# Loading K of the second attention unit in two halves, in a sliding-window attention kernel on one core

## The chip, the cores and the metric

The kernel runs on one core of one Trainium2 chip. The metric is the device time of one execution in microseconds; lower is better. Four runs of the kernel before gave 184.63, 184.4, 185.11 and 186.37 us, median 184.87 us.

## The reference, cut to what matters

```python
B, Sq, D = 8, 32, 1024
Hq, Hkv, Sk, Dh = 32, 4, 8192, 128
W = min(4096, max(256, Sk // 4))            # 2048: only the last W keys are used
rep = Hq // Hkv                             # 8 query heads share one K/V head
q = (x @ wq).reshape(B, Sq, Hq, Dh).transpose(0, 2, 1, 3)
k = repeat(k_cache[:, :, Sk - W:, :], rep, axis=1)
v = repeat(v_cache[:, :, Sk - W:, :], rep, axis=1)
scores = einsum("bhqd,bhkd->bhqk", q, k) * Dh ** -0.5
p = softmax(scores, axis=-1)
o = einsum("bhqk,bhkd->bhqd", p, v)
return o.transpose(0, 2, 1, 3).reshape(B, Sq, Hq * Dh) @ wo
```

All inputs are bfloat16. The K and V that are used come to 32 pairs of 2048 x 128, 512 KB each.

## The kernel before, in words

**Units.** One unit is one batch row b and one K/V head g; there are 32, head by head, so units 0 to 7 are the eight batch rows of head 0. A unit has 256 query rows (8 heads times 32) and 2048 keys, cut into 16 tiles of 128 keys. It is worked in four chunks of four key tiles. A chunk is four matmuls for scores (`s_ps`, L504), one exponential on ScalarE (`pT`, L506), and eight matmuls of the probabilities with V (`o_ps`, L515). The V tile `va` carries a column of ones, so that the sum of the softmax comes out of the same matmuls. The V matmuls of a chunk are issued two chunks after its scores. Four chunks of 32 units give 128 slots; other work is dealt out to slots: the query projection of later heads (`q_ps`, L285, and `ql_ps`, L301), the output projection (`op_ps`, L322) and the turning of some K.

**K must be turned.** The scores need K with Dh on the partitions (`kT`). There are three ways. Units 0, 1 and 2 (`PE_T`) load K as it lies into `k_raw` and turn it on TensorE (L397 for unit 0, `tp` at L244 for units 1 and 2); VectorE copies each half of eight tiles out of PSUM (L401, L246). Units in `V_T` (4, 7, 9, 12 and so on) load K as it lies and turn it with VectorE block transposes (`kb`, L259) and block moves on VectorE and GpSimd (`kTv`, L268 and L270). All others use a transposing DMA, in two halves (L200). In this text K1 is K of unit 1, V1 is V of unit 1, and so on; wq is the query weight.

**Where K1 is turned.** The pieces for K1 are placed among the chunks of unit 0: the first half (tiles 0 to 7) after the scores of chunk 2, the second half after those of chunk 3. K2's pieces lie in unit 1, after chunk 1, 2 and 3.

**Loads.** All loads but one half of x are issued by SyncE's queue, in the order of the program. `start` writes the first of them out by hand: x, six pieces of wq with the two halves of K0 among and behind them, V0, K1, V1, K2, K4, V2, and then unit 3: first half of K3, V3, second half of K3. From then on `load_unit` is called at a slot for each unit.

**Completion semaphores.** In the program as it is built, DMAs take eight completion semaphores in turn, and a DMA that reuses one waits on the issuing queue until the transfer that had it before has landed. So every DMA waits for the transfer eight issues before it, and everything behind it in SyncE's queue waits too. In the kernel before, V1 waits for the fourth piece of wq, K2 for the fifth, K4 for the first half of K0, V2 for the sixth piece of wq, the first half of K3 for the seventh, V3 for the second half of K0, and the second half of K3 for V0.

**Copies of V.** V lands in `v_sb` and is copied into one of three `va` buffers: for units 1 and 2 by GpSimd (L437), for all others by VectorE (L439).

**VectorE's order.** VectorE works in the order of the program. Around unit 1 it is: the two copies of K1 (L246), the first block transpose of K4 (L259), the closing of unit 0 (L445, L449, L451), the copy of K2's first half (L246), two more block transposes of K4, the copy of K2's second half, and so on.

Of the kernel before, what the change touches and what calls it, by code (L numbers as in the profile page):

```python
# [108 lines left out]
class Fast:  # L109
# [229 lines left out]
    def start(self):  # L339
# [14 lines left out]
        wq0[6]()  # L354
        self.load_k(0, 1)
        self.load_v(0, nc.sync)
        self.load_k(1)
        self.weights = []
        for g in range(self.Hkv):
            if g + 1 < self.Hkv:  # L360
# [333 lines left out]
```

## Time and profile before

| what | value |
|---|---|
| median of four runs | 184.87 us |
| the profiled execution, its own time | 184.98 us |
| its span in the profile | 183.2 us |
| PE busy | 178.0 us, 97% of the span |
| PEld busy | 152.8 us, 83% |
| ACT, DVE, POOL busy | 136.1, 125.5, 89.2 us |
| granted TensorE clock | 1.0 |
| data moved by DMA | 51.72 MB, mean 282 GB/s |
| the chain that ended last | PE 93%, DMA 4% |

The span is the time from the first to the last recorded instruction. The profiled execution took 1.78 us more than its span, and 0.11 us more than the median. PE is TensorE's matmuls, PEld its weight loads, DVE VectorE, ACT ScalarE, POOL GpSimd, SPq the queue of SyncE that issues DMAs. A DMA's row in the timeline is the time that its issuing takes; when the data has landed is told apart from it, as a time from issue to landing.

### The profile page before, as it was taken

Reading aid. Unit: us, or ns where it says so; the run is one execution under the profiler, and the core shown is the slowest. Engines: PE = TensorE matmul, PEld = TensorE weight load, DVE = VectorE, ACT = ScalarE, POOL = GpSimd, SP = SyncE. Lnnn points to the kernel's source line nnn. Section 1 sums busy time; section 2 is a strip of 40 time slices with the busy share of each in tenths; the row PEclk is TensorE's granted clock in tenths of the full one; section 3 lists DMA queues with packets and bytes.
Section 4 is the critical chain, followed back from the end, with each engine's and each line's share of the span. In section 5 each row is a group of like instructions: output and inputs, shape, how many; then the busy total and the mean of one; then the engine's idle time right before and its main releaser. Section 6 shows DMA issues by size and latency. Waiting matters only on the chain.

```text
span 183.2 us, 5015 instructions
## 1 busy us (share of the span) xinstructions
PE 178.0 (97%) x2026; PEld 152.8 (83%) x2041; DVE 125.5 (69%) x257; ACT 136.1 (74%) x146; POOL 89.2 (49%) x138
## 2 busy tenths in 40 slices
PE   8989999999999999999999999999999999999994
PEld 2879999999999999997878899988777788888843
DVE  0228799689887698477898656867587987554253
ACT  2218889888797888998787787788777788888800
POOL 2001665069880695945949706929705949600000
PEclk9999999999999999999999999999999999999999
DMA  5999999989999999999999997999999999970013
GB/s 187 320 407 406 231 378 381 245 261 261 363 393 253 358 262 342 381 281 324 292 381 246 415 359 257 383 243 354 277 302 275 339 292 338 209 176 0 0 32 89
DMA packets 52953, 51.72 MB, mean 282 GB/s; under 512 B 39744, under 2 KB 40256, under 8 KB 52928
## 3 DMA queue, kind: packets, MB, share of 16 engines
q1 hardware_dynamic: 52352, 50.90, 97.8%
q10 hardware_dynamic: 576, 0.49, 0.9%
q8 instruction: 15, 0.25, 0.5%
q14 instruction: 10, 0.08, 0.1%
HBM read 41.42 MB, written 0.52 MB: 229 GB/s over the span
## 4 chain that ended last, share of the span: by engine, by line
PE 93%; DMA 4%; SPq 1%; issue 1%; DVE 0%
PE o_ps L515 32%; PE s_ps L504 31%; PE op_ps L322 14%; PE q_ps L285 11%; DMA wq_sb<-in_wq_dram 4%; PE q_ps L405 2%; PE ql_ps L301 1%; PE tp L244 1%; SPq L168 1%; PE kf_ps L397 0%; SPq L347 0%; DVE o_t L332 0%; PE cnt_ps L570 0%
## 5 line engine op out<-in xcount | busy, mean ns | idle before, releaser
L506 ACT ACTIVATE pT<-s_ps 128x1024 bf16<-128x1024 f32 x128 | 128.4, 1027 | 26.8 <-PE s_ps L504 26.6
L270 POOL TENSOR_SCALAR kTv<-kb 32x512 bf16<-32x512 bf16 x126 | 84.5, 670 | 51.3 <-DVE kb L259 33.1
L515 PE MATMUL o_ps<-va,pT 128*128 128x129 bf16 x1024 | 78.8, 220 | 0.1
L515 PEld LDWEIGHTS <-pT 128*128 128x128 bf16 x1024 | 68.5, 98 | 3.1
L504 PE MATMUL s_ps<-QT,kT 128*128 128x256 bf16 x336 | 50.4, 272 | 0.1
L504 PEld LDWEIGHTS <-kT 128*128 128x128 bf16 x336 | 31.9, 98 | 9.4
L322 PE MATMUL op_ps<-wo_sb,OT 128*128 128x512 bf16 (+2 forms) x129 | 32.9, 353 | 0.6
L259 DVE STREAM_TRANSPOSE kb<-k_raw 128x512 bf16<-128x512 bf16 x44 | 29.7, 691 | 1.2 <-DMA k_raw<-in_k_cache_dram 0.9
L285 PE MATMUL q_ps<-xT,wq_sb 128*128 128x256 bf16 x192 | 28.3, 273 | 0.0
L504 PE MATMUL s_ps<-QT,kTv 128*128 128x256 bf16 x176 | 26.4, 273 | 0.1
L439 DVE COPY va<-v_sb 128x2048 bf16<-128x2048 bf16 x30 | 25.1, 835 | 1.1 <-DMA v_sb<-in_v_cache_dram 0.6
L445 DVE RECIPROCAL RL_all<-o_ps 128x2 f32<-128x2 f32 x32 | 5.3, 166 | 27.7 <-PE o_ps L515 27.3
L268 DVE COPY kTv<-kb 32x512 bf16<-32x512 bf16 x50 | 22.6, 452 | 1.2
L504 PEld LDWEIGHTS <-kTv 128*128 128x128 bf16 x176 | 17.0, 98 | 6.1
L285 PEld LDWEIGHTS <-wq_sb 128*128 128x128 bf16 x192 | 16.9, 98 | 1.2
L451 DVE STREAM_TRANSPOSE OT<-o_sb 128x256 bf16<-128x256 bf16 x32 | 14.3, 446 | 1.1
L449 DVE TENSOR_TENSOR o_sb<-o_ps,RL_all 128x256 bf16<-128x256 f32 x32 | 13.6, 424 | 1.1
L322 PEld LDWEIGHTS <-OT 128*128 128x128 bf16 x144 | 11.3, 98 | 2.3
L437 POOL TENSOR_SCALAR va<-v_sb 128x2048 bf16<-128x2048 bf16 x2 | 3.8, 1897 | 17.8 <-DMA v_sb<-in_v_cache_dram 17.8
L288 ACT CAST QT<-q_ps 128x512 bf16<-128x512 f32 x12 | 7.0, 582 | 0.2 <-PE q_ps L285 0.2
L405 PE MATMUL q_ps<-xT,wq_sb 128*128 128x256 bf16 (+1 forms) x64 | 6.0, 247 | 0.8 <-DMA wq_sb<-in_wq_dram 0.8
L329 DVE TENSOR_TENSOR oacc<-op_ps,oacc 128x512 f32<-128x512 f32 x8 | 5.3, 662 | 2.0 <-PE op_ps L322 2.0
(35 smaller groups left out, 43.6 us busy)
## 6 DMA issues: line engine op xcount, KB each, us to landing
v_sb<-in_v_cache_dram SPq DMA_DIRECT2D x30, 512.0 KB, 6.7
wo_sb<-in_wo_dram SPq DMA_DIRECT2D x16, 512.0 KB, 6.5
wq_sb<-in_wq_dram SPq DMA_DIRECT2D x13, 512.0 KB, 6.9
k_raw<-in_k_cache_dram SPq DMA_DIRECT2D x13, 512.0 KB, 6.0
wq_sb<-in_wq_dram SPq DMA_DIRECT2D x6, 256.0 KB, 5.4
v_sb<-in_v_cache_dram SPq DMA_DIRECT2D x4, 256.0 KB, 4.6
kT<-in_k_cache_dram SPq DMA_TRANSPOSE x36, 7.1
k_raw<-in_k_cache_dram SPq DMA_DIRECT2D x2, 256.0 KB, 6.9
```

The source lines that it names most:

```text
L259: nc.vector.transpose(out=st["kb"][:, sl, :], in_=self.k_raw[ui][:, sl, :])
L268: nc.vector.tensor_copy(out=out, in_=in_)
L270: nc.gpsimd.tensor_scalar(out=out, in0=in_, scalar1=1.0, scalar2=1.0, op0=ALU.mult, op1=ALU.mult)
L285: nc.tensor.matmul(st[k][:, hl % 2, :], lhsT=self.wq_t[g, i][:, c % (DC // 2), hl * P:(hl + 1) * P], rhs=self.xT[:, c, :], start=(c == 0 a ...
L322: nc.tensor.matmul(ps[:, 0:w], lhsT=self.OT[:, gq, c, t * P:(t + 1) * P], rhs=self.wo_t[gq][:, c, n0:n0 + w], start=(k == 0), stop=(k == 7))
L405: nc.tensor.matmul(ps, lhsT=self.wq_t[0, c // H][:, c % H, h * P:(h + 1) * P], rhs=self.xT[:, c, 0:n], start=(c == 0 and h in (0, 2, 4)), ...
L439: self.nc.vector.tensor_copy(out=out, in_=in_)
L449: nc.vector.tensor_tensor(out=o_sb[:, :, :, :], in0=o_ps[:, :, 0:Dh].rearrange("p q (i c) -> p q c i", c=4), in1=rl[:, ui * QT_N:(ui + 1) ...
L451: nc.vector.transpose(out=self.OT[:, g * QT_N:(g + 1) * QT_N, :, b * self.Sq:(b + 1) * self.Sq], in_=o_sb[:, :, :, :])
L504: nc.tensor.matmul(s_ps[:, jj, :], lhsT=self.kT[ui][:, c * CJ + jj, :], rhs=q_u, start=True, stop=True)
L506: nc.scalar.activation(out=pT[:, :, :], in_=s_ps[:, :, :], func=ACT.Exp, bias=0.0, scale=self.scale)
L515: nc.tensor.matmul(o_ps[:, qt, 0:self.VW], lhsT=pT[:, jj, qt * P:(qt + 1) * P], rhs=va[:, j, 0:self.VW], start=(j == 0 and qt == 0), stop= ...
```

## The change

K1 is issued as two loads of 256 KB, tiles 0 to 7 and tiles 8 to 15, into the two halves of the same `k_raw` buffer. `load_k` already has the form with a part: K0 uses it.

```diff
@@ -354,7 +354,8 @@
         wq0[6]()
         self.load_k(0, 1)
         self.load_v(0, nc.sync)
-        self.load_k(1)
+        self.load_k(1, 0)
+        self.load_k(1, 1)
         self.weights = []
```

The code that turns K1 is not touched. In the built program the eight matmuls that turn the first half of K1 now wait for the first of the two loads alone, and those for the second half have a wait of their own for the second. SyncE's queue has one DMA more, so every DMA behind K1 takes the next semaphore in the turn: V1 now waits for what K2 waited for, K2 for what K4 waited for, and so on. The order of the instructions on all engines is otherwise the same.

## The prediction

> **What bounds the kernel now.** I read the table of busy time first, then the table of waits for PE and PEld, then the stretches of 1 us at the start, then SyncE's own timeline with the landing time of each load, and last VectorE's timeline around unit 1.
>
> ```profile
> PE 178.0 (97%) x2026; PEld 152.8 (83%) x2041; DVE 125.5 (69%) x257; ACT 136.1 (74%) x146; POOL 89.2 (49%) x138
> ...
> PE 93%; DMA 4%; SPq 1%; issue 1%; DVE 0%
> ```
>
> ```profile
> PE q_ps L405 <- DMA wq_sb<-in_wq_dram: 0.8, 1, 0.8
> PE warm_ps L375 <- PEq L678: 0.8, 1, 0.8
> ```
>
> PE is busy nearly all the time, and its list of waits has two lines: 0.8 us before the first instruction, and 0.8 us for a piece of wq. Nothing in it names k_raw, so PE never waited for K1. The stretches (window, clock, busy time of PE, PEld, DVE, ACT, POOL, clock, DMA share, GB/s) show where the second wait lies, and that DMA runs at its full rate while K1 is on its way:
>
> ```profile
> 9.00:10.00 1.00, 0.27 (x5) 0.10 (x2) 0.00 (x0) 0.00 (x0) 0.00 (x0) 1.00 1.05 401
> ...
> 16.00:17.00 1.00, 1.00 (x19) 0.99 (x18) 1.00 (x3) 1.00 (x2) 0.00 (x0) 1.00 1.00 389
> 17.00:18.00 1.00, 1.00 (x18) 0.97 (x16) 0.70 (x2) 0.75 (x2) 0.42 (x1) 1.00 1.00 401
> ```
>
> From 10.1 us on PE is full in every stretch that I read (to 45 us). So a microsecond of PE stall is a microsecond of time, and little can be won: at most the 0.8 us at 9 to 10 us, which waits for a piece of wq issued 4.3 us ahead of K1.
>
> Now the loads. SyncE's timeline (start, duration of issue, line):
>
> ```profile
> 7.40 0.55 SPq L197 DMA_DIRECT2D k_raw<-in_k_cache_dram  x1
> 8.41 0.33 SPq L208 DMA_DIRECT2D v_sb<-in_v_cache_dram  x1
> 10.09 1.01 SPq L197 DMA_DIRECT2D k_raw<-in_k_cache_dram  x2
> 11.43 0.33 SPq L208 DMA_DIRECT2D v_sb<-in_v_cache_dram  x1
> 12.12 1.35 SPq L200 DMA_TRANSPOSE kT<-in_k_cache_dram  x1
> 13.52 4.47 SPq L208 DMA_DIRECT2D v_sb<-in_v_cache_dram  x1
> 18.04 3.13 SPq L200 DMA_TRANSPOSE kT<-in_k_cache_dram  x1
> ```
>
> These are K1, V1, K2 with K4, V2, the first half of K3, V3, the second half of K3. The answer by tile, cut to the window of one issue, gives the time to landing of each; issue plus that is: V0 6.80 + 7.3 = 14.1; K1 7.40 + 7.9 = 15.3; V1 8.41 + 9.1 = 17.5; K2 10.09 + 8.6 = 18.7; K4 about 10.8 + 9.1 = 19.9; V2 11.43 + 9.8 = 21.2; half of K3 12.12 + 10.0 = 22.1. Of the 7.9 us of K1, only some 1.3 us is its own data (512 KB at 400 GB/s). The rest is queueing behind what was issued before.
>
> Last, who takes the data. In the timeline of all engines:
>
> ```profile
> 16.33 0.49 PEld L244 LDWEIGHTS <-k_raw 128*128 128x128 bf16 x8
> ...
> 17.58 1.90 POOL L437 TENSOR_SCALAR va<-v_sb 128x2048 bf16<-128x2048 bf16 x1 [16.01 <-DMA v_sb<-in_v_cache_dram]
> 17.66 0.49 PEld L244 LDWEIGHTS <-k_raw 128*128 128x128 bf16 x8
> ...
> 19.91 0.71 DVE L259 STREAM_TRANSPOSE kb<-k_raw 128x512 bf16<-128x512 bf16 x1 [0.85 <-DMA k_raw<-in_k_cache_dram]
> ...
> 21.54 0.65 DVE L246 COPY kT<-tp 128x1024 bf16<-128x1024 bf16 x1
> ```
>
> The two PEld rows turn the halves of K1. The brackets on the POOL row and the first DVE row say that the engine sat idle until a load landed: GpSimd for V1, VectorE for K4. These two have no slack of their own, so what counts is the slack behind them.
>
> **What the Trainium skill says.** (1) "Perfetto Trace Analysis", DMA Optimizations: splitting a load may let the work start sooner if the DMA engines are generally idle. Here their share is about 1.0 from 9 to 18 us, so the condition isn't met. (2) The same page, Per-instruction lifecycle, HWDGE: a DMA's recorded span is the issue, not the movement. The trace agrees: K1 has 0.55 us of issue and 7.9 us to landing. (3) "DMA: Bandwidth & Descriptors", Queues, rings and completion order: each DMA engine takes the descriptors of one ring in order. The landings agree: they come in the order of issue, 1.2 to 2.2 us apart for 512 KB. (4) Its section Issuing engines are not separate DMA queues says that the issue is usually small beside the transfer; the trace has 0.33 to 0.56 us for plain loads here, but 4.47 us for V3.
>
> **The change part by part.**
>
> K1's first half. It is issued at 7.40 as K1 was and carries half the data, so it lands about 0.65 us before 15.3, at 14.7 (K0's second half and the pieces of wq, also 256 KB, land 0.65 to 0.7 us apart). Its taker starts at 16.33 and is put there by PE's own order. Gain: 0.
>
> K1's second half. It takes V1's place in the turn of semaphores and so goes out at 8.41. By the order of the ring it lands at 15.3 to 15.4. If landing followed issue, it would be V1's 17.5 at most. Its taker starts at 17.66, so even that end costs 0 (0.16 us left). 128 rows of 2 KB instead of 4 KB: the 256 KB pieces keep the rate of the others, so 0.
>
> V1 moves from 8.41 to 10.09. At 10.09 the loads before it that have not landed are K0 (two halves), two pieces of wq, V0 and K1: four of 256 KB and two of 512 KB, 2 MB, 5 us at 400 GB/s. So the DMA engines never run dry, V1's turn comes when it did, and it lands at 17.5. The other end is K2's landing, which was issued at 10.09 before with the same data ahead and V1 besides: 18.7. GpSimd's copy of 1.90 us then ends at 20.7 instead of 19.48; the matmuls that need it start at 20.61. So 0 to 0.1 us; I take 0.
>
> K2 moves from 10.09 to about 10.8, K4 to 11.43, V2 to 12.12. By the order of the ring their landings stay (18.7, 19.9, 21.2). At the other end each lands as its successor did: K2 19.9, K4 21.2, V2 22.1. K2's turning starts at 19.89: 0. V2's copy, 1.90 us from 22.1, ends at 24.0, needed at 25.28: 0. K4 is the sore point, priced in the rival below: 0 to 1.0 us; I take 0, because issue-to-landing grew from 7.3 to 10.0 us as the queue grew, which is the mark of a queue that is served in order at a fixed rate.
>
> K3 and V3: the first half of K3 waits for the second half of K0 (6.22 + 6.6 = 12.8) instead of 12.12, V3 for V0 (14.1) instead of 13.52. V3's issue ran to 17.99; I read its 4.47 us as room for descriptors becoming free, which later starts do not move. If it is a fixed duration instead, all later loads come 0.6 us later. After that SyncE waits 8.2 us, in four waits between 18 and 60 us, for PE to release kT buffers, and PE waits for no load to the end, so this costs 0 to 0.6 us; I take 0. From the second half of K3 on the waits are for transfers long landed, or the same as before.
>
> The added DMA itself: one issue of 0.33 to 0.55 us on SyncE, at a time when SyncE only waits for a semaphore (7.95 to 8.41). The added wait on PE (second half of K1) and the added semaphores on the first kTv moves, at 24.6 us, are for loads landed long before: 0.
>
> Sum: 0 on 184.98 us, the time of the profiled execution. That lies 0.11 us above the median, so I give the median: 184.9 us.
>
> **The rivals.**
>
> *A, slower: VectorE stands behind K4.* Issue does set the landing, and K4 lands at 21.2 instead of 19.9. VectorE's first block transpose of K4 then starts 1.3 us later, and in its order follow unit 0's closing and the copy of K2's first half, which ended at 22.19 and ends at 23.5. PE loads those weights at 22.57 for the scores of unit 2, so PE stalls 0.9 to 1.0 us: 185.9 us. It decides from the point where K4 lands 0.4 us late (22.57 - 22.19), after about 20.3. For it: the 0.85 us that VectorE waits already. Against it: the ring's order. If K4 slips to the next landing but one, 22.1, it costs 1.85 us: 186.8 us.
>
> *B, slower: the stream stays late.* V3's 4.47 us is a fixed duration and 0.6 us stays: 185.5 us at most. Against it: SyncE's waits for PE.
>
> *C, faster: less data ahead of a piece that PE waits for.* V1 no longer joins the ring at 8.41. If the pieces of wq landed sooner for that, the wait at 9 to 10 us shrinks: at most 0.8 us, 184.1 us. Against it: that piece was issued at 3.08, ahead of all of this.
>
> **How the numbers follow.** Main case 0.58, 184.3 to 185.5. A 0.22, of which 0.10 lies over 186.7. B, with other loads that stay late, 0.07, of which 0.03 over 186.7. C 0.05, none of it over 1%, since it can give 0.8 us at most. Unseen 0.08, half on each side, counted as over 1%. About 1% (1.85 us) is what a measurement of this kernel can tell from no change; its four runs spread by 1.97 us. So faster 0.04, slower 0.10 + 0.03 + 0.04 = 0.17, within 1% the rest, 0.79. The range runs from C's 184.1 to A's worse end, 186.9.
>
> **What would show it.** In the profile after, SyncE issues K1 at 7.4 and 8.4, V1 near 10.1, K4 near 11.4. Right: the GpSimd copy of V1 starts near 17.6, VectorE's first block transpose of K4 near 19.9, V3's issue ends near 18.0, and PE's list of waits is the same two lines. Wrong: a PE wait for DVE kT L246 near 22.6 (rival A), a wait for k_raw or va before it, or a gap in PE after 26 us.

## The result, and the profile after

| kernel | median | runs | ratio to before, 95% interval |
|---|---|---|---|
| before | 184.9 us (184.12 to 186.87) | 63 | 1 |
| after | 185.82 us (184.99 to 187.81) | 42 | 1.0047 (1.0034 to 1.006) |

The change makes the kernel 0.87 us slower (0.0047 times 184.9 us; 0.63 to 1.11 us by the interval). That is inside the 1% that the prediction took for "no change that a measurement can tell", and inside its range, but it is not the 0 of its main case, and it lies above the 184.3 to 185.5 us of that case: over 105 runs a loss of half a per cent can be told from nothing.

The profiled execution of the kernel after took 187.37 us with a span of 185.6 us. It is one of the long ones, because its last two outputs of 32 KB took 3.7 and 3.5 us to land, where the kernel before has 1.5 us for both. So its span is not set against that of before; the stretches ahead of the outputs are.

The table of busy time and the engines of the chain, as shown of before:

```profile
PE 177.7 (96%) x2026; PEld 152.6 (82%) x2041; DVE 125.5 (68%) x257; ACT 136.2 (73%) x146; POOL 89.1 (48%) x138
...
PE 90%; DMA 4%; SPq 1%; issue 1%; DVE 1%
```

The work is the same. The list of waits for PE, and the lines of PEld and of SyncE's queue that matter below:

```profile
PE q_ps L406 <- DMA wq_sb<-in_wq_dram: 1.0, 1, 1.0
PE warm_ps L376 <- PEq L679: 0.8, 1, 0.8
PE s_ps L505 <- DVE kTv L268: 0.2, 1, 0.2
```

```profile
PEld L505 <- POOL kTv L270: 0.3, 1, 0.3
```

```profile
SPq L690 <- DMA out_dram<-o_t: 3.6, 1, 3.6
```

The first two lines of PE are those of before. The third is new: PE waits for `kTv`, K turned by block moves, which has nothing to do with K1. SyncE's timeline where the change was made:

```profile
6.78 0.52 SPq L197 DMA_DIRECT2D k_raw<-in_k_cache_dram  x1
7.89 0.33 SPq L192 DMA_DIRECT2D k_raw<-in_k_cache_dram  x1
9.77 0.33 SPq L208 DMA_DIRECT2D v_sb<-in_v_cache_dram  x1
10.44 0.99 SPq L197 DMA_DIRECT2D k_raw<-in_k_cache_dram  x2
11.79 0.33 SPq L208 DMA_DIRECT2D v_sb<-in_v_cache_dram  x1
12.47 5.32 SPq L200 DMA_TRANSPOSE kT<-in_k_cache_dram  x1
17.85 0.57 SPq L208 DMA_DIRECT2D v_sb<-in_v_cache_dram  x1
18.47 2.65 SPq L200 DMA_TRANSPOSE kT<-in_k_cache_dram  x1
```

The two halves of K1 go out at 6.78 and 7.89, V1 at 9.77, K2 and K4 from 10.44, V2, the first half of K3, V3, the second half of K3. The long issue moved from V3 (4.47 us before) to the transposing DMA ahead of it (5.32 us); V3 is issued from 17.85 to 18.42 and not from 13.52 to 17.99, and the next load after K3 starts at 21.16 (21.21 before). Issue plus time to landing gives 14.42 and 15.09 for the halves of K1, 17.30 for V1, 18.58 for K2 and 19.84 for K4 (before: 15.34 for all of K1, then 17.50, 18.64 and 19.89). The takers, in the timeline of all engines:

```profile
17.38 1.90 POOL L438 TENSOR_SCALAR va<-v_sb 128x2048 bf16<-128x2048 bf16 x1 [15.81 <-DMA v_sb<-in_v_cache_dram]
...
19.86 0.71 DVE L259 STREAM_TRANSPOSE kb<-k_raw 128x512 bf16<-128x512 bf16 x1 [1.12 <-DMA k_raw<-in_k_cache_dram]
...
21.49 0.65 DVE L246 COPY kT<-tp 128x1024 bf16<-128x1024 bf16 x1
```

V1, K4 and the copy of K2's first half stand at 17.38, 19.86 and 21.49, against 17.58, 19.91 and 21.54 before. The loads are 0.05 to 0.2 us ahead there. PE is 0.3 us ahead, because its wait for the fifth piece of wq ended at 9.80 us and not at 10.11; over the 14 profiles of this document PE goes on with that piece at 8.83 to 10.19 us.

**Where the time goes.** VectorE closes each unit with one reciprocal (L445 before, L446 after); the distances between their starts don't depend on when the execution began. Three stretches of it:

| from, to | before | after |
|---|---|---|
| closing of unit 4 to closing of unit 12 | 39.92 us | 39.93 us |
| closing of unit 12 to closing of unit 17 | 24.83 us | 25.09 us |
| closing of unit 17 to closing of unit 31 | 71.65 us | 71.65 us |

0.26 us are lost in the middle stretch, and inside it in one place: the closing of unit 13 comes 4.27 us after that of unit 12 (3.93 before), and the next makes up 0.08. What stands there is PE's start on unit 14, at 80.38 us of the profile after. PE's timeline of before and then of after (the bracket is idle time and what ended it):

```profile
79.93 0.62 PE L515 MATMUL o_ps<-va,pT 128*128 128x129 bf16 x8
80.41 0.60 PE L504 MATMUL s_ps<-QT,kTv 128*128 128x256 bf16 x4
```

```profile
79.61 0.62 PE L516 MATMUL o_ps<-va,pT 128*128 128x129 bf16 x8
80.38 0.60 PE L505 MATMUL s_ps<-QT,kTv 128*128 128x256 bf16 x4 [0.16 <-DVE kTv L268]
```

The `kTv` that it waits for is filled in 16 block moves, 12 of GpSimd and four of VectorE; GpSimd's start after VectorE's fourth block transpose. Both rows of before, then both of after:

```profile
70.44 0.71 DVE L259 STREAM_TRANSPOSE kb<-k_raw 128x512 bf16<-128x512 bf16 x1
...
71.33 8.73 POOL L270 TENSOR_SCALAR kTv<-kb 32x512 bf16<-32x512 bf16 x12 [1.93 <-DVE kb L259]
```

```profile
70.12 0.71 DVE L259 STREAM_TRANSPOSE kb<-k_raw 128x512 bf16<-128x512 bf16 x1
...
71.36 8.73 POOL L270 TENSOR_SCALAR kTv<-kb 32x512 bf16<-32x512 bf16 x12 [2.28 <-PE q_ps L285]
```

Before, GpSimd starts 0.18 us after the transpose ends (71.33 less 70.44 and 0.71); after, 0.53 us. Its 12 moves end at 80.06 before and at 80.08 after, and PE's first load of weights from `kTv` comes 0.27 us behind that in both (80.33 and 80.35): before, PE arrived just then, so these moves had no slack. VectorE's last move ends 0.15 us after GpSimd's last in both kernels, which is why PE's row names VectorE. All other units that are turned this way start 0.14 to 0.19 us after their transpose in both kernels.

The bracket of the last row names PE as the releaser. That is the last semaphore that was raised before the start, and not what held GpSimd up: its wait is a row of its own in the trace, and it is done at 71.23 us before and at 70.91 after, 0.08 us after the transpose ends in both. The 0.35 us lie between the end of that wait and the start of the move.

**Why GpSimd starts late there.** The built program has, beside SyncE's one DMA more, one instruction more on GpSimd, and none more on PE, VectorE or ScalarE. `kTv` of unit 7 takes the buffer in which K1 lay, so its first block move has to wait until K1 has landed, and after the change that is two semaphores instead of one. In the built program these are:

```text
before:  wait (K1, VectorE)                                      first block move of unit 7
after:   wait (K1, one half)   wait (K1, other half, VectorE)    first block move of unit 7
```

At 37.85 us both halves are long there, so the wait itself costs nothing. But from there on every instruction of GpSimd stands one place further on in its list: the first block move of unit 14 stands at 68 instead of 67, counted from 0.

**The end.** The other part lies behind the last closing. Before, the span ends 7.99 us after the closing of unit 31 (183.2 less 175.21). The profile after has long outputs there, so the kernel after was run again, in the first experiment.

### The profile page after: what moved, and what is told of

The parts are those of the page before. It is cut to its first block, busy times and chain, and to the rows that moved or that the text cites. A ratio compares the mean times of both kernels' runs of the same rounds, so it can differ in the third digit from the quotient of the medians.

```text
span 185.6 us, 5017 instructions
## 1 busy us (share of the span) xinstructions
PE 177.7 (96%) x2026; PEld 152.6 (82%) x2041; DVE 125.5 (68%) x257; ACT 136.2 (73%) x146; POOL 89.1 (48%) x138
## 4 chain that ended last, share of the span: by engine, by line
PE 90%; DMA 4%; SPq 1%; issue 1%; DVE 1%
PE o_ps L516 31%; PE s_ps L505 30%; PE op_ps L322 14%; PE q_ps L285 11%; DMA wq_sb<-in_wq_dram 4%; PE q_ps L406 2%; PE tp L244 1%; PE ql_ps L301 1%; SPq L168 1%; PE kf_ps L398 0%; DVE kTv L268 0%; DVE o_sb L450 0%; SPq L347 0%; DVE o_t L332 0%; DVE RL_all L446 0%
## 5 line engine op out<-in xcount | busy, mean ns | idle before, releaser
L446 DVE RECIPROCAL RL_all<-o_ps 128x2 f32<-128x2 f32 x32 | 5.3, 166 | 27.2 <-PE o_ps L516 27.0
```

## The experiments

The theories: (1) one place further on in GpSimd's list costs what is lost at unit 14; (2) the shift of the turn of semaphores costs something at the end of the program; (3) the prediction's rival A, VectorE standing behind K4, costs something at the start. The rival to all three is that cutting K1 costs by itself. "Shifted early" says that all DMAs from K1's place on take the next semaphore in the turn.

### The kernel after, again

No edit.

> The changed kernel once more, for a second profile. All theories: about 0.9 us slower than before (185.7 to 185.9 us). They differ in where the profile has it. Start theory (a load that lands late stalls PE near unit 1 or 2): the closing of unit 2 on VectorE, at 30.9 us before, comes 0.5 us or more later against the first scores. Middle theory (the stream of loads keeps coming late, block moves of K are late for PE): the closings of units 12 to 31 come later by 0.5 us or more. End theory: the closings come as before within 0.1 us, and the span grows after the last VectorE instruction at 180.5 us: the last output transfers land later or the end of the program is longer.

185.67 us, ratio 1.005 (1.0028 to 1.0071). Closing of unit 12 to 17: 25.10 us. Its start has rival A:

```profile
19.99 0.71 DVE L259 STREAM_TRANSPOSE kb<-k_raw 128x512 bf16<-128x512 bf16 x1 [1.70 <-DMA k_raw<-in_k_cache_dram]
...
22.33 0.61 PE L505 MATMUL s_ps<-QT,kT 128*128 128x256 bf16 x4 [0.32 <-DVE kT L246]
```

Here PE had got its wq sooner and was ahead, K4 was not, VectorE stood 1.70 us for K4, and PE lost about half a microsecond (0.49 us by PEld's row). From PE's going on with the fifth piece of wq to the closing of unit 3 it is 24.31 us here, and 23.82 us in the profile of before: these 0.49 us are lost. The execution had gone on with wq 0.77 us sooner than that of before (9.34 and 10.11 us), so it still is 0.28 us ahead when unit 3 closes (33.66 and 33.94 us).

The end: 8.44 us from the closing of unit 31 to the end of the last instruction, 0.45 more than before. (The trace gives both to 0.01 us; the span on the page is rounded to 0.1.) The outputs are issued at the same distances and land in the same times (1.5 us for the two of 32 KB). What differs is the waits of SyncE's queue for them; the line of the kernel before, then of this run (in total, times, longest):

```profile
SPq L689 <- DMA out_dram<-o_t: 1.0, 3, 0.4
```

```profile
SPq L690 <- DMA out_dram<-o_t: 1.6, 1, 1.6
```

The built program ends with eight waits on SyncE, one for each completion semaphore, in the order of their numbers. Before, the last two outputs have the last two semaphores, so that the other waits are done while they are on their way. With one DMA more in the program they have the last and, around the turn, the first: SyncE stands at the first of its eight waits until the very last output has landed, and then goes through seven more. The trace has each wait as a row. The eight of the kernel before, then of this run (count, shortest, median and longest in ns, first and last start):

```profile
L689 SPq EVENT_SEMAPHORE  x8: 28/28/28, 180.8 to 182.3; - x8
```

```profile
L690 SPq EVENT_SEMAPHORE  x8: 28/28/28, 182.3 to 182.8; - x8
```

The last output lands at 182.31 before and at 182.30 here. Before, the eighth wait starts at 182.32, and no other wait follows it; here the first starts at 182.32 and the eighth at 182.76, each 0.06 to 0.07 us after the one ahead of it. These 0.44 us are the loss at the end. The first profile of the kernel after has the same eight rows behind its late outputs, from 184.27 to 184.71.

### An unused small load right after K1, and the same load late

```diff
+    def dummy(self):
+        self.nc.sync.dma_start(out=self.dum[:, :], in_=self.v_cache[0, 0, 0:self.P, 0:64])
...
         self.load_k(1)
+        self.dummy()
```

> K1 in one load as before, and behind it one more load of 16 KB that nobody uses. The turn of the eight semaphores is shifted as in the changed kernel, and V1, K2, K4 and V2 wait for what they wait for there; K1 is not cut. If the shifted turn makes the loss (start, middle or end theory), 0.7 to 1.0 us slower than before. If cutting K1 itself makes it (descriptors of 2 KB, the second half later), 0 to 0.2 us.

184.99 us, ratio 1.0011 (0.9988 to 1.0033). In the second kernel the same load stands ahead of unit 30's loads instead:

> As before, with one more load of 16 KB that nobody uses ahead of the loads of unit 30, near 150 us. All that comes earlier is untouched; the last loads and the outputs take the next semaphore in the turn, and SyncE has one instruction more. End theory: 0.7 to 1.0 us slower than before, like the changed kernel. Start and middle theories: no difference (within 0.2 us).

185.16 us, ratio 1.0019 (0.9995 to 1.0044). Neither has unit 14's loss (24.83 and 24.82 us between the closings of 12 and 17), and both have the end's: 8.44 us behind the closing of unit 31. So the shift, early or late, costs at the end. By time alone neither can be told from before, and the early one is not slower than the late one; both stay short of the 0.7 to 1.0 us that were expected if the shift made the whole loss. The profile of the early one has a loss of 0.4 us at unit 7, which lies in the landing of a V near 37 us.

### V1 between the halves of K1

```diff
         self.load_k(1, 0)
-        self.load_k(1, 1)
...
         self.load_v(1, nc.sync)
+        self.load_k(1, 1)
```

> K1 in two loads, but V1 between them: V1 waits for what it waited for before the change, K1's second half goes out behind it; K2, K4 and all that follows as in the changed kernel. Start theory with V1 as the late load: back to the time before (within 0.2 us). Start theory with K4, middle and end theories: 0.7 to 1.0 us slower than before.

185.99 us, ratio 1.0062 (1.0029 to 1.0096). Here V1 keeps its semaphore. The loss is that of the change or more: 25.09 us between the closings of units 12 and 17, 8.44 us at the end. V1's delay is not the cause.

### GpSimd's list one instruction longer, and one shorter

To the kernel before, K1 whole, one small memset is added at the start:

```diff
         nc.gpsimd.memset(self.ones_c[:, :], 1.0)
+        nc.gpsimd.memset(self.dum[:, :], 1.0)
```

> The kernel before, with one more instruction on GpSimd at the start (one column of a tile that nobody reads is set, off the path); loads and their turn are untouched. The cut of K1 puts one more instruction on GpSimd's queue too, a wait, and in the profiles of the three kernels with K1 cut the first block move for unit 14 starts 0.5 us after its data is there instead of 0.2 us, and PE loses 0.35 us at unit 14. If that comes from GpSimd's instructions standing one place further on: the same 0.35 us at the closing of unit 13, and 0.2 to 0.5 us slower than before. If it comes from the wait itself or from the loads: no difference (within 0.2 us).

185.07 us, ratio 1.0027 (1.0005 to 1.0048). In its profile:

```profile
69.87 0.71 DVE L260 STREAM_TRANSPOSE kb<-k_raw 128x512 bf16<-128x512 bf16 x1
...
71.11 8.73 POOL L271 TENSOR_SCALAR kTv<-kb 32x512 bf16<-32x512 bf16 x12 [2.28 <-PE q_ps L286]
```

That is 0.53 us again, 25.09 us between the closings, and 7.99 us at the end. A memset at the start, 70 us earlier, gives unit 14's loss whole. From the kernel after one is taken away:

```diff
-        nc.gpsimd.memset(self.ones_c[:, :], 1.0)
...
-        nc.tensor.matmul(cnt[0:1, 0:2 * ncol], lhsT=self.ones_c[:, :], ...)
+        nc.tensor.matmul(cnt[0:1, 0:2 * ncol], lhsT=nc.const_aps.tensor(1.0, [P, 1], BF16), ...)
```

> The changed kernel, with one instruction less on GpSimd at the start (the column of ones for the last check comes from the program's constants), so that from unit 7 on GpSimd's instructions stand where they stood before. If the place of the instructions costs the 0.35 us at unit 14: closing 13 keeps the distance that closing 12 has, and the time is 185.2 to 185.5 us, 0.3 to 0.5 us less than the changed kernel. If not: as the changed kernel, 185.7 us.

185.06 us, ratio 1.0027 (1.0003 to 1.0051). GpSimd starts unit 14 0.18 us after the transpose again, 24.83 us between the closings, and the end's loss stays: 8.45 us. The time is below the 185.2 to 185.5 us expected; the kernel before was lower in this group of runs too (184.58 us), and the ratio is the one to go by.

### VectorE not behind K4

```diff
-V_T = {4: (None, (4, 6, 6, 7), 8, 13, 8),
+V_T = {4: (None, (6, 6, 6, 7), 8, 13, 8),
```

The kernel after, with K4's first block transpose placed behind the copy of K2's first half, so that it can't hold that copy up.

> The changed kernel, with the first block transpose of K4 moved from slot 4 to slot 6, so that on VectorE the closing of unit 0 and the copy of K2's first half no longer stand behind K4's landing. If K4's late landing stalls PE at unit 2 in many executions (rival A): no PE wait for the copy of K2 and 0.1 to 0.5 us less than the changed kernel, 185.2 to 185.6 us; the loss at unit 14 stays. If K4 has no part: as the changed kernel.

185.64 us, ratio 1.0052 (1.003 to 1.0075). Nothing is won that can be measured: rival A is no large part of the loss. In the profile PE has no wait for K2's copy, but from its going on with the fifth piece of wq to the closing of unit 3 it still takes 23.91 us, 0.09 more than before. The middle stretch is 25.09 us, the end 8.53 us.

### The kernel before, again

> The kernel before once more, for a second profile: K4 lands 9.7 to 9.9 us after PE resumes with the fifth piece of wq (9.80 in the first profile, 10.06 to 10.65 in the kernels with the shifted turn), no loss at closing 13, and no PE wait but the two of the first profile. If the distance scatters up to 10.6 here too, the turn isn't what moves K4.

184.49 us in its one run. Its profile repeats that of before in all three marks: 24.83 us, 8.00 us at the end, and no wait for `kTv`. K4's first transpose starts 9.82 us after PE goes on with the fifth piece of wq, as expected.

### Both parts mended, and the end alone

`V_HALVES` says from which unit on V is loaded in two halves. Set to 31, unit 30's V is one load, and the last outputs have the semaphores that they had before. Both start from the kernel after. The first has this and the instruction taken from GpSimd as above; the second has this alone.

```diff
-V_HALVES = 30
+V_HALVES = 31
```

> The change with both suspected costs taken away: unit 30's V comes as one load instead of two halves, so that the turn of semaphores is back where it was for the last outputs, and GpSimd has one instruction less (the column of ones of the mask counts is taken from the kernel's constants), so that its moves stand where they stood. Theory of two causes: the same as the kernel before, ratio 0.999 to 1.002; closing of unit 12 to that of 13 3.93 us, span behind the closing of unit 31 about 8.0 us. If a third part comes from the start (VectorE behind K4), 0.2 to 0.5 us stay over the kernel before (1.001 to 1.003). If the two causes are no causes: 1.005, as the change has it.

185.23 us, ratio 1.0021 (1.0 to 1.0042).

> The change with unit 30's V as one load: the turn of semaphores is shifted from K1 on but not for the last outputs, GpSimd keeps the added instruction. Theory of two causes: the end's 0.45 us goes (about 8.0 us behind the closing of unit 31), unit 14's 0.35 us stays (4.27 us between the closings of units 12 and 13): ratio about 1.002. If the end costs nothing, 1.005 as the change.

185.08 us, ratio 1.0017 (0.9997 to 1.0037). In the profiles both ends are as before, 7.99 us, and the middle stretch is 24.83 us in the first and 25.09 us in the second, as the theory has it. By time the second is where it was expected; the first is just past the upper edge of what was expected of two mended parts and in the field of the third (1.001 to 1.003), though its interval starts at no loss. Its profile lost 0.33 us between the closings of units 5 and 6, where VectorE stood 0.57 us for a V near 37 us, as in the run with the early unused load.

### Both parts added to the kernel before

The late unused load and the added memset together; K1 is whole and nothing moves at the start.

> The kernel before, K1 whole, with an unused load of 16 KB late (ahead of unit 30's loads) and one more small memset on GpSimd at the start. Theory of two causes: the whole loss of the change without its cut: ratio 1.004 to 1.005, 4.27 us between the closings of units 12 and 13, about 8.45 us behind the closing of unit 31. If the loss belongs to the cut of K1 or to the shift early on: 1.000 to 1.002.

185.79 us, ratio 1.0046 (1.0026 to 1.0066): the loss of the change, without the change. 25.09 us between the closings, 8.44 us at the end.

### Fourteen more instructions on GpSimd

```diff
+        for i in range(14):
+            nc.gpsimd.memset(self.dum[:, :], 1.0)
```

> The kernel before with 14 more small memsets on GpSimd at the start. In the list of GpSimd's instructions the first block move of unit 14 stands at 67 before and at 68 in the change; here it stands at 81, and that of unit 12 stands at 68. If it is the place in the list that makes a first move late: unit 12's starts 0.53 us after its last block transpose, unit 14's 0.18 us, as before, and PE has no wait at unit 14 (3.93 us between the closings of units 12 and 13); ratio 0.999 to 1.002, plus what unit 12 may lose, up to 0.35 us. If any added instruction makes unit 14's first move late, whatever its place: 0.53 us at unit 14 again and 4.27 us.

184.74 us, ratio 0.9985 (0.9969 to 1.0001), just under the 0.999 to 1.002 expected. Now it is the moves of unit 12 that start late, and those of unit 14 that start at once:

```profile
58.98 0.67 DVE L260 STREAM_TRANSPOSE kb<-k_raw 128x512 bf16<-128x512 bf16 x1
...
60.17 8.73 POOL L271 TENSOR_SCALAR kTv<-kb 32x512 bf16<-32x512 bf16 x12 [6.65 <-PE s_ps L507]
```

```profile
69.57 0.71 DVE L260 STREAM_TRANSPOSE kb<-k_raw 128x512 bf16<-128x512 bf16 x1
...
70.46 8.73 POOL L271 TENSOR_SCALAR kTv<-kb 32x512 bf16<-32x512 bf16 x12 [1.55 <-DVE kb L260]
```

60.17 less 58.98 and 0.67 is 0.52 us, at the move that now stands at 68; 70.46 less 69.57 and 0.71 is 0.18 us. Unit 12's moves have slack: PE has no wait for `kTv`, and the middle stretch is 24.83 us. So it is the place in the list that makes a first move late, and the unit that happens to stand there decides whether that costs anything. The memset of one instruction and these 14 use the same new tile, so it is not the tile either. Why GpSimd takes 0.35 us longer at that place was not found out. One thing in the traces moves with it: the DMA queue that the page lists as `q14 instruction` has a transfer of 8 KB 1.8 to 3.3 us after instruction 68 starts in the 13 other profiles, at 72.6 to 75.1 us, and here 4.0 us after it, at 64.2 us, while its other transfers stay within some 1 us of where the other profiles have them. That hints at the engine's supply of instructions; no run tests it.

### The sum

| kernel | closings of units 12 to 17 | behind the closing of unit 31 |
|---|---|---|
| before, and again | 24.83, 24.83 us | 7.99, 8.00 us |
| after again, V1 between, VectorE not behind K4 | 25.10, 25.09, 25.09 us | 8.44, 8.44, 8.53 us |
| memset more; end mended | 25.09; 25.09 us | 7.99; 7.99 us |
| unused load early, late; memset less | 24.83, 24.82; 24.83 us | 8.44, 8.44; 8.45 us |
| both mended; 14 memsets | 24.83; 24.83 us | 7.99; 7.99 us |
| both added | 25.09 us | 8.44 us |

In each column the kernels fall into two groups with nothing between, and each is in the group that its edit says. The profiles so give 0.26 us for GpSimd's place and 0.45 us for the end (0.54 in one), 0.7 to 0.8 us of the 0.87 us measured; the rest is within the interval of 0.63 to 1.11 us. The times agree: the twelve ratios to the kernel before, fitted by one cost for each part (least squares, each weighted by its interval), give 0.44 us ± 0.21 for the place, 0.36 us ± 0.23 for the end, and 0.09 us ± 0.22 for all that an early shift does. Kernels that ran together share their runs of the kernel before, so these intervals are not independent.

Open stays whether the early shift costs anything at all. Four profiles have rival A's stall, with 0.08 to 0.49 us, and one of the four is of a kernel whose turn isn't shifted (14 memsets, 0.12 us). Three have a V that landed late at 37 us, with 0.42, 0.33 and 0.14 us, and the last of them, both parts added, has no early shift either. The time of the kernel with both parts mended (0 to 0.8 us over before) leaves room for a cost of the early shift; the fit puts it at 0.3 us at most.

## Why the prediction was right, and where it wasn't

**The number owes something to luck.** 185.82 us lies above the range of the main case and next to the 185.9 us of rival A, which is not its cause. It stayed within 1% because two costs that the prediction didn't have come to 0.7 us; nothing in its argument bounded them.

**The reading of the start held.** The prediction's main case was that each load lands as before by the order of the ring. The halves of K1 were foreseen at 14.7 and 15.3 to 15.4 and landed at 14.42 and 15.09, V1's copy was foreseen at 17.6 and started at 17.38, K4's transpose at 19.9 and 19.86. V3's issue was to end near 18.0 and ended at 18.42, which the load behind it made up. The 4.47 us of V3 were no duration of V3: the long issue went to the DMA ahead of it and ended at 17.79. Room in the ring, as the prediction has it, fits that; no run shows it by itself. That the added issue costs SyncE nothing (7.89 to 8.22, in a wait) held too. And nothing was won, because no one waited for K1 and the DMA engines were full (a share of 1.00 to 1.09 in each microsecond from 9 to 18, before and after): the condition that the Trainium skill sets for a split load ("Perfetto Trace Analysis", DMA Optimizations), engines that are generally idle, was not met, and the runs agree with it.

**Rival A is real, but it doesn't need the change.** What decides it is not K4's landing alone but how far PE has got. The prediction set the point at K4 0.4 us late. From PE's going on with the fifth piece of wq (of seven that `start` issues, not six) to K4's first transpose it is 9.80 us before (10.11 to 19.91), so a stall should begin at some 10.2 us. In the profile after it is 10.06 us (9.80 to 19.86): 0.26 us of the slack are gone, and no stall. In the repeated run it is 10.65 us, and PE lost 0.49 us; with V1 between the halves, with 14 memsets and with the early unused load it is 10.29, 10.28 and 10.23 us, and PE lost 0.13, 0.12 and 0.08 us; in the others it is under 10.2, and nothing was lost (VectorE not behind K4 is left out here). So the 0.38 us of slack that the prediction reckoned with held to 0.03 us, with a smaller price than the 0.9 to 1.0 us of a K4 that is 1.3 us late. But the kernel with 14 memsets has K1 whole and its loads in the old turn: there PE had its wq early (9.12 us), and that was enough. That the shifted turn makes K4 later is not shown: the distance is 9.57 to 10.28 us in six profiles with the old turn and 9.77 to 10.65 us in seven with the shifted one.

**The first step that failed: the added semaphores at 0.** The prediction said "the added semaphores on the first kTv moves, at 24.6 us, are for loads landed long before: 0". That asked how long the wait lasts, which is indeed nothing. It didn't ask what the wait is in the built program: for unit 7's first move, one more instruction on GpSimd, which sets all that follow one place further on. Measured: 0.35 us at unit 14, where GpSimd's 12 moves, 8.73 us in all, had no slack; 0.26 us of it stay.

**The second: "the same as before" to the end.** The prediction followed the shifted turn of semaphores through SyncE's loads and stopped when the waits there cost nothing. The turn goes on to the last output, and there the program waits for all eight in the order of their numbers. Measured: 0.45 us, seven waits of 0.06 to 0.07 us behind the last landing. SyncE's list of waits of the kernel before had the line that leads there, the wait for `out_dram` in three pieces of 0.4 us at most; of SyncE's waits the prediction speaks of those up to 60 us alone.

Both lie outside the window that the prediction watched. It named "a gap in PE after 26 us" as a mark of error, and that is what came, at 80 us; no rival described it. The 0.08 for the unseen was its place, though the prediction took the unseen to be over 1%, and it came to half of that.

## What to carry to other kernels

Splitting a load where nobody waits for it wins nothing, and its cost is to be looked for far from the split: in the buffer's next tenant, which gets one wait more, and in everything that counts DMAs. Follow a shifted turn of semaphores to the last output, and read the waits at the end of the program as one reads those in the middle. When a loss of a few tenths appears where nothing was changed, compare distances between fixed events of the program (here the closings of units) and not clock times: within each group of the table they repeated to 0.02 us in all profiles but one, where medians of twenty runs resolve some 0.4 us.

## What the runs showed of the hardware that was not expected

A GpSimd instruction that follows a wait started 0.52 to 0.53 us after its releaser instead of 0.18 us when it stood at one certain place in the engine's list of instructions (68, counted from 0, in seven kernels), whether it belonged to unit 14 (six kernels) or to unit 12 (one); at the places that the other first moves had in these kernels it was 0.14 to 0.19 us. The wait itself was done 0.08 us after the releaser in either case.

And waits that are already fulfilled are not free: SyncE's eight at the end stand 0.06 to 0.07 us apart, so that seven of them behind the last landing make the end 0.44 us longer (182.32 to 182.76 us in the repeated run, 184.27 to 184.71 in the first profile after).
